# Loads of a fused attention and mixture-of-experts kernel in quarter pieces behind single exponentials, with row stores, list building and one ratio at other units

## The chip, the cores and the metric

One core of one Trainium2 chip. The time is in device microseconds of one execution of the program; lower is better.

## The reference

Attention over 8 batches of 8 heads, 576 positions, 64 dimensions, with rotated q and k; then, with the attention output as 4608 rows of 512, a top-1 mixture of 8 experts. Cut to what matters:

```python
q_rot, k_rot = rotate(q), rotate(k)
scores = scale * q_rot @ k_rot.T
attn = exp(scores - max(scores)); attn /= attn.sum(-1) + 1e-09
x = (attn @ v).transpose(0, 2, 1, 3).reshape(B * S, H * D)
e_idx = argmax(x @ w_gate)                    # one expert for each row
probs = softmax(x @ w_gate); eom = sigmoid(x @ w_output_gate)
out[row] = probs[row, e] * eom[row, e] * (relu(x[row] @ w1[e]) @ w2[e])   # e = e_idx[row]
```

## The kernel before, in words

All inputs are float32. The attention runs over 32 pairs of heads, four for each batch, numbered 0 to 31. A pair has nine units: eight of 128 query rows by one head and one that holds the last 64 rows of both heads. The order of the work is written out by hand as a table of numbers: entry `(name, o, k)` of pair n runs at unit 9n + o, after that unit's exponentials, in place k among those of its unit. No scheduler reorders anything; each engine takes its instructions in the order in which the code issues them.

For a unit, PE makes the scores (tile `sc`, L521), DVE finds the row peak (`peak`, L530, tile `pm`), ACT takes the exponential (`exp`, L537), and DVE transposes (L543, L545, tile `pt`). PE multiplies with the values (`values`, L567, tile `acc`, 144 products for a pair, run one pair later), ACT copies the sums out of PSUM (L574 to L576), PE turns them back (`back`, L582), and DVE divides (`divide`, L594, tile `xb`), which ends the pair's part of one batch's rows. There is one `acc` tile of four PSUM banks.

A pair's inputs come by DMA over SP's queue: `load(1)` and `load(0)` bring the k and the q side of q, k and their half-swapped copies (tile `raw`, 576 KB each, two tiles in turn), `loadv(0)` and `loadv(1)` the values of each head (tile `v`, 576 KB each, two in turn). SP issues a DMA as soon as its tile is free, so the place in the table only sets the order. POOL rotates: two multiplications (`mult`, L472), an addition (`add`, L476), and, after ACT's rounded copy (`high`, L482), the rest (`low`, L485), which completes tile `kq` for the scores two pairs after the loads were due.

After a batch's last pair, `place` routes its rows: POOL sums the gate logits, ACT takes an exponential `eg` (L679) for the ratio by which a row is weighted (s10, s11, s12, s13), PE counts rows in front of each row (s14, L715, in bank 3 of a later pair's `acc`, the "guest" sums), ACT copies the counts out (`rc`, L720), and POOL works out list row and place of each token (s14b to s17: `pr`, `po`, `hr`, `lo`). From these ACT makes row and place matrices (`ones`, tile `ro`, L761 and L762; `places`, tile `pl`, L772 and L773) at the units of `ROWS` and `PLACES`, and PE multiplies them into lists (s20, also in bank 3, columns from 128 on), which ACT copies out (`lc`, L720). Batches 0 to 3 are of kind "free", 4 "late", 5 (the last but two) "early", 6 "ahead"; batch 7 is done in the expert phase. The finished rows go to DRAM (`store`, tile `xd`) over SP's queue, from where the expert phase gathers them.

The expert phase starts near 472 us. Its weights (tile `wr`, 512 KB each, L1098) come over the same SP queue behind the last `loadv`.

The lines of the tables that the change edits:

```python
PREPARED = [("load1", -18, 1), ("load0", -15, 1), ("mult1", -14, 1), ("mult0", -11, 1), ...]
ROWS = {"early": (26, 29, 31, 35, 40), "late": (28, 33, 38, 42, 49), "free": (29, 38, 47, 51, 56), ...}
PLACE = 20   # an entry (o, k) of place runs at unit 9 * (last pair of the batch) + PLACE + o
```

Of the kernel before, what the change touches and what calls it, by code (L numbers as in the profile page):

```python
# [64 lines left out]
ROWS = {"ahead": (26, 29, 29, 31, 31), "early": (26, 29, 31, 35, 40), "late": (28, 33, 38, 42, 49), "free": (29, 38, 47, 51, 56)}  # L65
PLACES = {"ahead": (26, 27, 28, 29, 30), "early": (25, 29, 31, 34, 38), "late": (29, 31, 40, 47, 51), "free": (33, 40, 42, 49, 58)}
# [209 lines left out]
class Attention:  # L276


    def __init__(self, tc, nb, pools, cc, ident, ii, first, trib, oneb, cnt, zero, qk, v, xd, row, lists):
# [33 lines left out]
        for i, pr in enumerate(self.pairs):  # L313
            g, b = 9 * i, i // NP
            fs = {"lasts": pr.lasts, "den0": pr.den0, "den1": pr.den1, "den2": pr.den2, "evict": pr.evict, "back": pr.back,
                  "newxb": lambda pr=pr, b=b: newxb(b) if pr.hp == 0 else None}
            fs["divide"] = lambda pr=pr, b=b: pr.divide(xbs[b])
            for t, n in ((slice(0, 1), "0"), (slice(1, 2), "1"), (slice(0, 2), "")):
                fs[f"mult{n}"] = lambda pr=pr, t=t: pr.mult("P", t)
                fs[f"add{n}"] = lambda pr=pr, t=t: pr.add("P", t)  # L320
                fs[f"hi{n}"] = lambda pr=pr, t=t: pr.high(t)
                fs[f"lo{n}"] = lambda pr=pr, t=t: pr.low("P", t)
            for t in range(2):
                fs[f"load{t}"] = lambda pr=pr, t=t: pr.load(t)
                fs[f"loadv{t}"] = lambda pr=pr, t=t: pr.loadv(t)
# [76 lines left out]
class Pair:  # L402
# [49 lines left out]
    def load(self, t):  # L452

        if t:
            self.raw = self.pp2.tile([P, 4, S], F32, tag="raw", name=f"raw{self.nm}")
        self.nc.sync.dma_start(out=self.raw[:, 2 * t:2 * t + 2, :], in_=self.qkd[:, 2 * t:2 * t + 2, :])

    def loadv(self, t):
# [3 lines left out]
        self.nc.sync.dma_start(out=self.v[:, t, :, :], in_=self.vd[:, t, :, :])  # L462
# [31 lines left out]
    def begin(self):  # L494
        self.pc, self.ps, self.m = {}, {}, {}
# [36 lines left out]
    def exp(self, i):  # L532
# [4 lines left out]
        self.nc.scalar.activation(self.pc[i], self.pc[i], AF.Exp, bias=self.m[i], scale=-1.0, accum_out=self.z[:, zi:zi + 1])  # L537
# [51 lines left out]
    def divide(self, xb):  # L589
# [4 lines left out]
        self.divided = self.nc.vector.tensor_tensor(out=heads(xb[:, :, x0:x0 + BW]), in0=heads(acc), in1=rz.broadcast_to((P, NCH, HW, 2)),  # L594
                                                    op=ALU.mult)
        for m in self.guests:
            self.apart(self.divided, m)

    def apart(self, a, b):

        self.tc.declare_no_dep(a.ins, b.ins, reason="the products stand in banks 0 and 1, the guests' sums in bank 3")

    def guest(self, m):
        self.guests.append(m)


def place(tc, pools, pairs, b, NT, cc, trib, oneb, cnt, xbs, xd, row, lists, tops, later):
# [100 lines left out]
    def psum(k, at, n):  # L708
# [3 lines left out]
        return host.acc[:, 3, at:at + n]  # L712

    def summed(*a, **k):
        m = nc.tensor.matmul(*a, skip_group_check=True, **k)  # L715
        if not last:
            T["host"].guest(m)

    def taken(out, a):
        T["host"].guest(nc.scalar.copy(out, a))  # L720

    def s14():

        rk = T["rk"] = psum(2, 0, (NCH + 1) * E).rearrange("p (a b) -> p a b", b=E)
# [71 lines left out]
    if last:  # L796
# [543 lines left out]
```

## Time and profile before

| | us |
|---|---|
| median of 3 runs | 965.22 |
| the runs | 961.87, 965.65, 965.22 |
| the profiled execution | 961.01 |
| its span | 959.2 |
| PE busy in the span | 911.8 |
| DVE, ACT, POOL busy | 753.4, 658.7, 528.9 |

The span is what the profile's engines cover; the execution's own time is 1.8 us longer. Busy times are sums over instructions; PE's ends are modelled. The profiled execution lies 4.2 us under the median.

### The profile page before, as it was taken

The numbers are of one execution on the slowest core, as the hardware profiler recorded it, in microseconds if no ns is written. First come the engines' busy times: TensorE is split into PE (matmuls) and PEld (weight loads), VectorE is DVE, ScalarE is ACT, GpSimd is POOL, SyncE is SP. The second block draws the span as 40 slices with busy tenths as digits, with TensorE's granted clock in tenths as the row PEclk, the third lists the DMA queues.
The fourth block names the chain that finished last, engine by engine and source line by source line (L and its number), as shares of the span: only waits on it lengthen the run. The fifth ranks groups of instructions, "written<-read, shape, count | busy, mean of one in ns | idle before, by whom it ended". The sixth has DMA issues, their size and how long they took to land.

```text
span 959.2 us, 34178 instructions
## 1 busy us (share of the span) xinstructions
PE 911.8 (95%) x14445; PEld 789.2 (82%) x14445; DVE 753.4 (79%) x1354; ACT 658.7 (69%) x1373; POOL 528.9 (55%) x483
## 2 busy tenths in 40 slices
PE   4999999999999989989899999999999999999997
PEld 3777777878878777777788998999899998999986
DVE  6899999999999989989588776657765757668562
ACT  4777789899998988797764544457645656556562
POOL 5898898898989898797222222142514315042140
PEclk9999999999999999999999999999999999999999
DMA  6554466365636555554299867667876868768560
GB/s 239 199 180 147 178 227 231 142 227 200 245 135 243 203 182 182 177 186 173 97 359 313 304 205 239 219 217 270 290 269 226 292 199 303 255 225 289 198 203 25
DMA packets 57821, 208.42 MB, mean 217 GB/s; under 512 B 7818, under 2 KB 8252, under 8 KB 57664
## 3 DMA queue, kind: packets, MB, share of 16 engines
q1 hardware_dynamic: 49920, 183.78, 54.8%
q0 software_dynamic: 6464, 21.26, 5.9%
q8 instruction: 115, 1.88, 0.8%
q10 hardware_dynamic: 1280, 1.15, 0.4%
q14 instruction: 42, 0.34, 0.1%
HBM read 186.09 MB, written 22.43 MB: 217 GB/s over the span
## 4 chain that ended last, share of the span: by engine, by line
PE 69%; DVE 13%; issue 6%; POOL 5%; ACT 5%; DMA 2%; POOLq 0%; DVEq 0%; SPq 0%; ACTq 0%
PE py L1192 20%; PE ph L1150 19%; PE acc L567 12%; PE sc L521 10%; DVE pm L530 6%; PE ph L1142 3%; DVE pt L545 2%; ACT pm L537 2%; PE acc L582 2%; POOL raw L472 2%; DVE pt L543 2%; PE mtp L1115 2%; POOL kq L485 1%; DVE xb L594 1%; DMA out<-y,2idx 1%
## 5 line engine op out<-in xcount | busy, mean ns | idle before, releaser
L537 ACT ACTIVATE pm<-pm,m 128x576 f32<-128x576 f32 x288 | 221.7, 770 | 55.9 <-DVE pm L530 52.6
L1109 DVE TENSOR_TENSOR wl<-wr,wh 128x1024 fp32r<-128x1024 f32 x172 | 216.2, 1271 | 37.2 <-ACT wh L1107 34.2
L530 DVE TENSOR_SCALAR_CACHE_REDUCE pm<-sc 128x576 f32<-128x576 f32 x288 | 205.1, 744 | 24.4 <-PE sc L521 19.4
L567 PE MATMUL acc<-pt,v 32*64 32x128 f32 (+1 forms) x9216 | 198.5, 295 | 21.2 <-issue 9.2
L1192 PE MATMUL py<-wh,ht 128*128 128x512 f32 x640 | 214.0, 400 | 0.0
L1150 PE MATMUL ph<-xt,wh 128*128 128x256 f32 x1088 | 198.3, 284 | 0.0
L567 PEld LDWEIGHTS acc<-pt,v 32*64 32x64 f32 x9216 | 157.5, 131 | 47.6 <-issue 29.7
L1107 ACT CAST wh<-wr 128x1024 fp32r<-128x1024 f32 x184 | 187.8, 1049 | 0.0
L521 PE MATMUL sc<-kq 64*128 64x288 f32 x1536 | 159.8, 320 | 15.4 <-ACT kq L482 9.6
L1150 PEld LDWEIGHTS ph<-xt,wh 128*128 128x128 f32 x1088 | 169.8, 190 | 2.6 <-DVE xt L1131 1.2
L472 POOL TENSOR_TENSOR raw<-raw,rt 128x1152 f32<-128x1152 f32 x62 | 164.8, 2658 | 0.0
L521 PEld LDWEIGHTS sc<-kq 64*128 64x128 f32 x1536 | 121.5, 190 | 48.7 <-issue 20.8
L1150 PE MATMUL ph<-xt,wl 128*128 128x256 f32 x544 | 154.0, 283 | 0.0
L1192 PEld LDWEIGHTS py<-wh,ht 128*128 128x128 f32 x640 | 120.3, 188 | 25.2
L1192 PE MATMUL py<-wl,ht 128*128 128x512 f32 x320 | 125.8, 393 | 0.0
L543 DVE STREAM_TRANSPOSE pt<-pm 128x576 f32<-128x576 f32 x160 | 116.7, 759 | 2.1 <-ACT pm L537 2.1
L1166 ACT ACTIVATE ht<-ph 128x512 fp32r<-128x512 f32 x68 | 40.7, 598 | 112.9 <-PE ph L1150 103.3
L1197 POOL DMA_INDIRECT out<-y,2idx x24 | 26.0, 1083 | 166.1 <-ACT y L1206 104.7
L1167 DVE SCALAR_TENSOR_TENSOR ht<-ph,ht 128x512 fp32r<-128x512 f32 x68 | 47.0, 691 | 73.7 <-ACT ht L1166 70.3
L1150 PEld LDWEIGHTS ph<-xt,wl 128*128 128x128 f32 x544 | 103.0, 189 | 0.2 <-DVE wl L1109 0.2
L545 DVE STREAM_TRANSPOSE pt<-pm 128x1152 f32<-128x1152 f32 x64 | 87.9, 1373 | 0.7 <-ACT pm L537 0.7
L485 POOL TENSOR_TENSOR kq<-raw,kq 128x1152 fp32r<-128x1152 f32 (+1 forms) x33 | 82.8, 2509 | 8.7 <-ACT kq L482 8.5
(243 smaller groups left out, 1105.0 us busy)
## 6 DMA issues: line engine op xcount, KB each, us to landing
wr<-in_w SPq DMA_DIRECT2D x184, 512.0 KB, 4.4
raw<-in_qk SPq DMA_DIRECT2D x64, 576.0 KB, 5.2
v<-in_v SPq DMA_DIRECT2D x64, 576.0 KB, 6.1
xd<-xb SPq DMA_DIRECT2D x16, 640.0 KB
xd<-xb SPq DMA_DIRECT2D x8, 160.0 KB, 5.1
rt<-in_rope ACTq DMA_DIRECT2D x1, 576.0 KB
xg<-xd,2idx POOLq DMA_INDIRECT x24, 6.7
out<-y,2idx POOLq DMA_INDIRECT x24, 3.4
```

Source lines behind the costliest of these rows:

```text
L472: self.eng(eng).tensor_tensor(out=rv, in0=rv, in1=rt, op=ALU.mult)
L485: self.eng(eng).tensor_tensor(out=self.sides(self.kq, t, 0, x), in0=self.sides(self.raw, t, 0, x), in1=self.sides(self.kq.bitcast(F32), t, ...
L521: self.nc.tensor.matmul(self.ps[i][:, a, :HS], st, self.kq[r, mov, x], start=(n == 0), stop=(n == 2))
L530: self.nc.vector.tensor_scalar(self.halves(i), self.ps[i][:, :, :HS], 1.0, FAR, op0=ALU.mult, op1=ALU.min, accum_out=self.m[i])
L537: self.nc.scalar.activation(self.pc[i], self.pc[i], AF.Exp, bias=self.m[i], scale=-1.0, accum_out=self.z[:, zi:zi + 1])
L543: self.nc.vector.transpose(out=self.pt[:, c + 5 * h, :], in_=self.pc[units[0]])
L545: self.nc.vector.transpose(out=self.pt[:, c:c + 6:5, :], in_=self.pc[units])
L567: nc.tensor.matmul(self.acc[h * D:h * D + D, a, o:o + 32 * n], self.v[r, h, j, :], self.pt[r, u:u + n, 32 * j:32 * j + 32], start=(j == 0) ...
L1107: self.nc.scalar.copy(wh, r)
L1109: eng.tensor_tensor(out=wl, in0=r, in1=wh.bitcast(F32), op=ALU.subtract)
L1150: nc.tensor.matmul(ph[:, f, :], st[:, dc, fs], mv[:, dc, :], start=(n == 0), stop=(n == 11))
L1192: self.nc.tensor.matmul(py[h], st[:, f, hs], mv, start=(f == 0 and n == 0), stop=(f == 7 and n == 2))
```

## The change

Loads: `raw` and `v` now come in four pieces of 288 KB each in place of two of 576 KB. Piece t of pair n's `raw` waits for the exponential of unit t of pair n - 2 (k side first), piece t of its `v` for the exponential of unit t + 4 of pair n itself. The three row stores of a batch stand together at PLACE + 33, between a pair's last `v` piece and the next `raw` pieces, and the ratio is written into the rows (s13) at PLACE + 24 in one instruction in place of two. One `ro` chunk of the "free" batches moves from 51 to 31, `pl` chunks of "late" from 47 and 51 to 45 and 47, those of "early" to other units. The lists' sums stand in PSUM bank 2, the counts in bank 3, and the two are declared independent. For batch 5 POOL works out `pr`, `po`, `hr` and `lo` directly after the counts and the ratio behind them.

```diff
+LOADED = [(f"load{t}", t - 18, 2) for t in range(4)]
+PREPARED = [*LOADED, ("mult1", -14, 1), ("mult0", -11, 1), ("add", -9, 1), ("hi", -6, 1), ("lo", -5, 2)]
 EVENTS = [
-    ("lasts", 1, 2), ("loadv0", 5, 2), ("loadv1", 7, 2),
+    ("lasts", 1, 2), *[(f"loadv{t}", t + 4, 2) for t in range(4)],
...
-ROWS = {"ahead": (26, 29, 29, 31, 31), "early": (26, 29, 31, 35, 40), "late": (28, 33, 38, 42, 49), "free": (29, 38, 47, 51, 56)}
-PLACES = {"ahead": (26, 27, 28, 29, 30), "early": (25, 29, 31, 34, 38), "late": (29, 31, 40, 47, 51), "free": (33, 40, 42, 49, 58)}
+ROWS = {"ahead": (26, 29, 29, 31, 31), "early": (22, 24, 29, 33, 38), "late": (28, 33, 38, 42, 49), "free": (29, 31, 38, 47, 56)}
+PLACES = {"ahead": (26, 27, 28, 29, 30), "early": (22, 27, 31, 35, 40), "late": (29, 31, 40, 45, 47), "free": (33, 40, 42, 49, 58)}
...
+                fs[f"load{t}"] = lambda i=i, pr=pr, t=t: pr.load(t, self.pairs[i - 2].ex[t])
+                fs[f"loadv{t}"] = lambda pr=pr, t=t: pr.loadv(t, pr.ex[t + 4])
...
+    def behind(self, dma, ex):
+        if ex is not None:
+            info = mybir.DependencyInfo(mybir.DependencyClass.Sync, mybir.DependencyReason.DATA)
+            self.tc.add_manual_dep(dma.ins, ex.ins.name, info, reason="transfers evenly in time")
+    def load(self, t, ex=None):
+        if t == 0:
             self.raw = self.pp2.tile([P, 4, S], F32, tag="raw", name=f"raw{self.nm}")
-        self.nc.sync.dma_start(out=self.raw[:, 2 * t:2 * t + 2, :], in_=self.qkd[:, 2 * t:2 * t + 2, :])
+        t ^= 2
+        self.behind(self.nc.sync.dma_start(out=self.raw[:, t, :], in_=self.qkd[:, t, :]), ex)
...
-    def guest(self, m):
-        self.guests.append(m)
+    def guest(self, m, bank):
+        for o, k in self.guests:
+            if k != bank and o.ins.engine != m.ins.engine:
+                self.apart(m, o)
+        self.guests.append((m, bank))
...
-        rk = T["rk"] = psum(2, 0, (NCH + 1) * E).rearrange("p (a b) -> p a b", b=E)
+        rk = T["rk"] = psum(2, 3, (NCH + 1) * E).rearrange("p (a b) -> p a b", b=E)
...
-        T["ls"] = psum((listed + PLACE) // 9 - 2, 128, lists.shape[1])
+        T["ls"] = psum((listed + PLACE) // 9 - 2, 2, lists.shape[1])
...
+    ratio = lambda: (s10(), s11())
+    if early:
+        fs += [(18, 2, s14b), (18, 2, s15), (19, 2, s16), (19, 2, s17), (20, 2, ratio), (22, 2, s12)]
+    else:
+        fs += [(19, 2, ratio), (19, 2, s14b), (20, 2, s15), (21, 2, s12), (22, 2, s16), (23, 2, s17)]
...
-        fs += [(29, 2, lambda: gated(0, 2)), (33, 2, lambda: store(0)), (38, 2, lambda: gated(2, NCH)),
-               (42, 2, lambda: store(1)), (42, 2, lambda: store(2))]
+        fs += [(24, 2, s13), (33, 2, lambda: store(0)), (33, 2, lambda: store(1)), (33, 2, lambda: store(2))]
```

SP's queue around the row stores of batch 0. Before, a transfer waits only for its tile (`Pool`: POOL has finished with the `raw` tile, `PE`: the values before are used) and for the semaphore of an earlier transfer (`DMAHW`); a tile's number is the program's own:

```order
L462 DMA v_2469<-in_v 128x1152 [waits DMAHW3_49,DMAHW2_49,PE_49]
L462 DMA v_2469<-in_v 128x1152
L700 DMA xd<-xb_584 128x2x640 [waits DMAHW4_49,Pool_49]
L456 DMA raw_2575<-in_qk 128x1152 [waits DMAHW5_49,Pool_49]
L456 DMA raw_2575<-in_qk 128x1152 [waits DMAHW6_49]
L462 DMA v_2760<-in_v 128x1152 [waits DMAHW7_49,PE_49]
L462 DMA v_2760<-in_v 128x1152 [waits DMAHW0_49]
L700 DMA xd<-xb_584 128x2x640 [waits DMAHW1_49,Pool_49]
```

and after, where `Activation` is the exponential:

```order
L472 DMA v_2437<-in_v 128x576 [waits DMAHW0_49,Activation_49]
L472 DMA v_2437<-in_v 128x576 [waits DMAHW1_49,Activation_49]
L713 DMA xd<-xb_594 128x2x640 [waits DMAHW2_49,Pool_49]
L713 DMA xd<-xb_594 128x2x640 [waits DMAHW3_49]
L715 DMA xd<-xb_594 64x640 [waits DMAHW4_49]
L465 DMA raw_2619<-in_qk 128x576 [waits DMAHW5_49,Activation_49,Pool_49]
L465 DMA raw_2619<-in_qk 128x576 [waits DMAHW6_49,Activation_49]
L465 DMA raw_2619<-in_qk 128x576 [waits DMAHW7_49,Activation_49]
```

What ran ahead on free tiles now waits for ACT piece by piece, and the three stores stand in one row.

PE at the unit where batch 4's lists (`ro`, `pl`) and batch 5's counts (`hot`) are summed. Before:

```order
L715 MATMUL acc_7682<-ro_7139,pl_7174 128x288 x4
L715 MATMUL acc_7682<-ro_7139,pl_7174 128x288 [waits Activation_49]
L715 LDWEIGHTS trib
L715 MATMUL acc_7682<-hot,trib 128x48 [waits Activation_49]
L715 LDWEIGHTS oneb
L715 MATMUL acc_7682<-hot,oneb 128x40
```

and after:

```order
L729 MATMUL acc_7787<-ro_7236,pl_7272 128x288 x5
L729 LDWEIGHTS trib
L729 MATMUL acc_7787<-hot,trib 128x48
L729 LDWEIGHTS oneb
L729 MATMUL acc_7787<-hot,oneb 128x40
```

The order is the same; the counts' wait for ACT (the copy `lc`) is gone, and so is that of the last list product for its `pl`.

POOL after batch 5's counts, the copy `rc`. Before:

```order
L737 TENSOR_TENSOR pr_8036<-rc_7962,base_7645 128x40
L738 TENSOR_TENSOR cnt<-rc_7962,cnt 128x8
L682 TENSOR_SCALAR eg_7990<-eg_7990 128x5
L685 TENSOR_TENSOR eg_7990<-eg_7990,so_7913 128x5
L792 TENSOR_TENSOR lists<-lists,lc_7954 128x288
L472 TENSOR_TENSOR raw_7940<-raw_7940,rt 128x1152
L741 TENSOR_TENSOR pr_8036<-pr_8036,hot 128x40
L485 TENSOR_TENSOR kq_8033<-raw_7641,kq_8033 128x2x576
```

and after:

```order
L755 TENSOR_TENSOR pr_8098<-pr_8098,hot 128x40
L643 TENSOR_TENSOR po_8146<-pr_8098 128x20
L643 TENSOR_TENSOR po_8148<-po_8146 128x10
L643 TENSOR_TENSOR po_8150<-po_8148 128x5
L763 TENSOR_SCALAR hr_8152<-po_8150 128x5
L764 TENSOR_SCALAR hr_8152<-hr_8152 128x5
L765 TENSOR_SCALAR hr_8152<-hr_8152 128x5
L766 TENSOR_SCALAR lo_8153<-hr_8152 128x5
L767 TENSOR_TENSOR lo_8153<-lo_8153,po_8150 128x5
L806 TENSOR_TENSOR lists<-lists,lc_8059 128x288
L482 TENSOR_TENSOR raw_8047<-raw_8047,rt 128x1152
L695 TENSOR_SCALAR eg_8096<-eg_8096 128x5
```

`lo` stood behind three large POOL instructions and the wait for ACT's `eg`; it now stands ahead of both.

## Rows read from the trace of the kernel before

**Rows 1.** windows between divides; PE, PEld, DVE, ACT, POOL busy, clock, DMA.

```profile
234.69:289.22 54.53, 52.33 (x1422) 43.46 (x1421) 52.95 (x112) 49.58 (x129) 49.96 (x46) 1.00 0.57 205
344.32:376.07 31.75, 27.52 (x714) 22.25 (x715) 26.83 (x57) 25.41 (x66) 28.29 (x23) 1.00 0.67 230
376.07:421.94 45.87, 40.50 (x1073) 33.12 (x1071) 40.11 (x85) 39.33 (x103) 37.84 (x43) 1.00 0.48 172
480.00:504.00 24.00, 24.00 (x161) 21.55 (x160) 19.75 (x36) 14.64 (x21) 4.96 (x4) 1.00 0.95 358
```

**Rows 2.** chain of work, two divides; start us, us, engine, tile, line.

```profile
71.51 0.89 DVE xb L594
...
84.89 0.89 DVE xb L594
```

**Rows 3.** waits of PE, 60 to 340 us; total us, times, longest.

```profile
PE acc L567 <- ACT rc L720: 3.5, 5, 0.8
...
PE acc L567 <- issue: 0.3, 1, 0.3
```

**Rows 4.** waits of PE from 340 to 425 us.

```profile
PE acc L567 <- issue: 6.1, 5, 1.5
...
PE acc L715 <- ACT lc L720: 1.2, 1, 1.2
```

**Rows 5.** page, part 3, instruction queue; packets, MB, share.

```profile
q8 instruction: 115, 1.88, 0.8%
```

**Rows 6.** DMA queues, 344 to 349 us.

```profile
q1 hardware_dynamic: 375, 1.54, 83.8%
```

**Rows 7.** DMA queues, 349 to 351 us.

```profile
q1 hardware_dynamic: 38, 0.14, 17.9%
q8 instruction: 1, 0.02, 3.0%
```

**Rows 8.** chain of work, 350 to 358 us.

```profile
350.95 0.85 issue
```

**Rows 9.** timelines of DVE, ACT; start us, us, instruction [idle <- who].

```profile
279.49 0.76 DVE L530 TENSOR_SCALAR_CACHE_REDUCE pm<-sc 128x576 f32<-128x576 f32 x1 [0.56 <-PE sc L521]
...
392.37 0.76 DVE L530 TENSOR_SCALAR_CACHE_REDUCE pm<-sc 128x576 f32<-128x576 f32 x1 [1.96 <-PE sc L521]
...
406.57 0.40 ACT L772 ACTIVATE pl<-row,lo 128x128 fp32r<-128x128 bf16 x1 [1.19 <-POOL lo L753]
```

**Rows 10.** waits of POOL from 24 to 336 us.

```profile
POOL eg L682 <- ACT eg L679: 10.0, 5, 2.3
...
POOL pr L737 <- ACT rc L720: 4.7, 5, 1.4
```

**Rows 11.** timelines, ACT (second exponential, pair 18), POOL (first multiplication, pair 20).

```profile
262.06 0.76 ACT L537 ACTIVATE pm<-pm,m 128x576 f32<-128x576 f32 x1
...
263.04 2.65 POOL L472 TENSOR_TENSOR raw<-raw,rt 128x1152 f32<-128x1152 f32 x1
```

**Rows 12.** page, part 6 (us to landing); one store, its window.

```profile
raw<-in_qk SPq DMA_DIRECT2D x64, 576.0 KB, 5.2
...
351.27 0.38 SPq L700 DMA_DIRECT2D xd<-xb  x1
...
352.00:354.20 2.20, 2.20 (x76) 1.81 (x73) 1.49 (x4) 1.98 (x7) 2.20 (x2) 1.00 0.79 297
```

**Rows 13.** end of the attention: timelines of SP and ACT, then the chain.

```profile
447.99 34.17 SPq L1098 DMA_DIRECT2D wr<-in_w  x10
...
459.34 0.78 ACT L537 ACTIVATE pm<-pm,m 128x576 f32<-128x576 f32 x1 [0.49 <-DVE pm L530]
...
468.33 2.95 ACT L1107 CAST wh<-wr 128x1024 fp32r<-128x1024 f32 x3
...
466.94 0.85 issue
...
470.21 1.87 issue
```

More of the change, by code (lines that the diff above doesn't have):

```diff
@@ L43 @@
 NB, TAIL, PE_ = S // 32, 160, 192
-PREPARED = [("load1", -18, 1), ("load0", -15, 1), ("mult1", -14, 1), ("mult0", -11, 1), ("add", -9, 1), ("hi", -6, 1), ("lo", -5, 2)]
+LOADED = [(f"load{t}", t - 18, 2) for t in range(4)]
+PREPARED = [*LOADED, ("mult1", -14, 1), ("mult0", -11, 1), ("add", -9, 1), ("hi", -6, 1), ("lo", -5, 2)]
 EVENTS = [
-    ("lasts", 1, 2), ("loadv0", 5, 2), ("loadv1", 7, 2),
+    ("lasts", 1, 2), *[(f"loadv{t}", t + 4, 2) for t in range(4)],
     ("av0", 12, 1), ("av1", 13, 0), ("av2", 14, 0), ("av3", 16, 0),
@@ L56 @@
     1: (("mult1", -9, 1), ("add1", -9, 1), ("mult0", -8, 1), ("add0", -7, 1), ("hi1", -5, 1), ("lo1", -4, 1), ("hi0", -3, 1), ("lo0", -2, 1)),
[1 row of a table removed]
+    2: (*LOADED, ("mult1", -11, 1), ("add1", -10, 1), ("mult0", -9, 1), ("add0", -7, 1), ("hi1", -6, 1),
         ("lo1", -5, 1), ("hi0", -4, 1), ("lo0", -3, 1)),
[1 row of a table removed]
+    3: (*LOADED, ("mult1", -11, 1), ("mult0", -9, 1), ("add", -7, 1), ("hi", -4, 1), ("lo", -4, 2)),
 }
@@ L322, in __init__ @@
                 fs[f"lo{n}"] = lambda pr=pr, t=t: pr.low("P", t)
-            for t in range(2):
-                fs[f"load{t}"] = lambda pr=pr, t=t: pr.load(t)
-                fs[f"loadv{t}"] = lambda pr=pr, t=t: pr.loadv(t)
+            for t in range(4):
+                fs[f"load{t}"] = lambda i=i, pr=pr, t=t: pr.load(t, self.pairs[i - 2].ex[t])
+                fs[f"loadv{t}"] = lambda pr=pr, t=t: pr.loadv(t, pr.ex[t + 4])
             for k, (b0, b1) in enumerate(PIECES):
@@ L357, in start @@
             f()
-        self.pairs[1].load(1)
-        self.pairs[1].load(0)
+        for t in range(4):
+            self.pairs[1].load(t)
         self.pairs[0].start()
@@ L450, in eng, with loadv @@
         return self.nc.gpsimd if eng == "P" else self.nc.vector
-    def load(self, t):
-        if t:
+    def behind(self, dma, ex):
[4 more added lines that the diff above has]
+        if t == 0:
             self.raw = self.pp2.tile([P, 4, S], F32, tag="raw", name=f"raw{self.nm}")
-        self.nc.sync.dma_start(out=self.raw[:, 2 * t:2 * t + 2, :], in_=self.qkd[:, 2 * t:2 * t + 2, :])
-    def loadv(self, t):
+        t ^= 2
+        self.behind(self.nc.sync.dma_start(out=self.raw[:, t, :], in_=self.qkd[:, t, :]), ex)
+    def loadv(self, t, ex):
         if t == 0:
             self.v = self.pa.tile([P, 2, NB, D], F32, tag="v", name=f"v{self.nm}")
-        self.nc.sync.dma_start(out=self.v[:, t, :, :], in_=self.vd[:, t, :, :])
+        h, j = t // 2, slice(t % 2 * 9, t % 2 * 9 + 9)
+        self.behind(self.nc.sync.dma_start(out=self.v[:, h, j, :], in_=self.vd[:, h, j, :]), ex)
     def sides(self, a, t, s, x):
@@ L494, in begin @@
     def begin(self):
-        self.pc, self.ps, self.m = {}, {}, {}
+        self.pc, self.ps, self.m, self.ex = {}, {}, {}, {}
         self.pt = self.pa.tile([P, 9, S], F32, tag="pt", name=f"pt{self.nm}")
@@ L536, in exp @@
             zi = 2 * c + h
-        self.nc.scalar.activation(self.pc[i], self.pc[i], AF.Exp, bias=self.m[i], scale=-1.0, accum_out=self.z[:, zi:zi + 1])
+        self.ex[i] = self.nc.scalar.activation(self.pc[i], self.pc[i], AF.Exp, bias=self.m[i], scale=-1.0, accum_out=self.z[:, zi:zi + 1])
     def turn(self, units):
@@ L593, in divide @@
         heads = lambda a: a.rearrange("p c (x h) -> p c x h", h=2)
[L594 to L597, printed above, removed]
+        divided = self.nc.vector.tensor_tensor(out=heads(xb[:, :, x0:x0 + BW]), in0=heads(acc), in1=rz.broadcast_to((P, NCH, HW, 2)),
+                                               op=ALU.mult)
+        for m, _ in self.guests:
+            self.apart(divided, m)
     def apart(self, a, b):
-        self.tc.declare_no_dep(a.ins, b.ins, reason="the products stand in banks 0 and 1, the guests' sums in bank 3")
-    def guest(self, m):
-        self.guests.append(m)
+        self.tc.declare_no_dep(a.ins, b.ins, reason="the products stand in banks 0 and 1, lists' sums in bank 2, counts in bank 3")
+    def guest(self, m, bank):
[3 more added lines that the diff above has]
+        self.guests.append((m, bank))
 def place(tc, pools, pairs, b, NT, cc, trib, oneb, cnt, xbs, xd, row, lists, tops, later):
@@ L705, in base, with psum @@
         tt(out=new("base", [P, E]), in0=cnt, in1=cc(C_EB), op=ALU.add)
-    def psum(k, at, n):
+    def psum(k, bank, n):
         if last:
@@ L711, in psum @@
         host = T["host"] = pairs[NP * b + NP - 1 + k]
-        return host.acc[:, 3, at:at + n]
+        T["bank"] = bank
+        return host.acc[:, bank, 0:n]
     def summed(*a, **k):
@@ L716, in summed @@
         if not last:
-            T["host"].guest(m)
+            T["host"].guest(m, T["bank"])
     def taken(out, a):
-        T["host"].guest(nc.scalar.copy(out, a))
+        T["host"].guest(nc.scalar.copy(out, a), T["bank"])
     def s14():
-        rk = T["rk"] = psum(2, 0, (NCH + 1) * E).rearrange("p (a b) -> p a b", b=E)
+        rk = T["rk"] = psum(2, 3, (NCH + 1) * E).rearrange("p (a b) -> p a b", b=E)
         mm = lambda out, st, mv, start, stop: summed(out, st, mv, start=start, stop=stop)
@@ L802, in place @@
     fs = [(0, 2, s0), (2, 2, s1), (2, 3, s2), (7, 2, base), (8, 2, s3), (10, 2, s4), (11, 2, s5), (12, 2, s7), (15, 2, s8), (17, 2, s14),
-          (17, 2, s14c), (19, 2, s14b), (18, 2, s9), (19, 2, lambda: (s10(), s11())), (20, 2, s15), (21, 2, s12), (22, 2, s16), (23, 2, s17)]
+          (17, 2, s14c), (18, 2, s9)]
+    ratio = lambda: (s10(), s11())
[3 more added lines that the diff above has]
+        fs += [(19, 2, ratio), (19, 2, s14b), (20, 2, s15), (21, 2, s12), (22, 2, s16), (23, 2, s17)]
     fs += [(listed, 2, s20), (listed, 2, s21), (listed + 1, 2, s22) if early else (listed + 2, 3, s22)]
```

2 rows, old and new, of the table PREP are left out of this document.

## The prediction

> **What bounds the kernel now.** I read the stretches first, then PE's waits, then the queues at each wait. Both phases run at the full clock [rows 1]: TensorE's granted clock is 1.00 of 2.4 GHz, so nothing here is a matter of the clock. From 480 to 504 us PE is busy in 24.00 of 24.00 us: the expert phase is bound by PE's own work, and the change adds nothing to that work and takes nothing from it. A gain or a loss must come from the attention, or from the change-over near 470 us.
>
> In the attention a pair takes 84.89 - 71.51 = 13.38 us where nothing is lost [rows 2]. An ordinary batch of four pairs takes 54.53 us, 13.63 a pair, with PE busy 52.33 and DVE 52.95 us: these two are nearly full. The five pairs from 344.32 to 421.94 take 31.75 + 45.87 = 77.62 us where five times 13.63 is 68.15 [rows 1]. So 9.5 us are lost in this stretch; PE is busy 27.52 + 40.50 = 68.0 of its 77.6 us. Where they go:
>
> - PE waits 6.1 us, in five waits of up to 1.5, for "issue", that is for nothing that the profile shows; from 60 to 340 us that was 0.3 us in all [rows 3, 4]. I take these for waits on PE's own instructions, which come by a DMA queue too: 115 packets and 1.88 MB in the run, 16 KB each [rows 5]. From 344 to 349 us the data queue alone fills 83.8% of the DMA engines and not one instruction packet moves; from 349 to 351 us, when the data fall to 17.9%, one does [rows 6, 7]; PE stops at 350.95 for 0.85 us, just as it has come in [rows 8].
> - PE waits 1.2 us to count rows into `acc`, for ACT's copy `lc` out of the same bank [rows 4]; DVE, which waits for the scores queued behind, is idle 1.96 us at 392.37 [rows 9].
> - ACT waits 1.19 us at 406.57 with a `pl` for POOL's `lo` [rows 9].
>
> 6.1 + 1.96 + 1.19 = 9.25, about the 9.5.
>
> **The change part by part.** The sum goes from the profiled execution, 961.0 us, and is moved to the median afterwards.
>
> Loads. The bytes stay. What changes is when they move: eight pieces of 288 KB behind one exponential each, in place of four transfers of 576 KB that start together as tiles come free. A 640 KB store issued by itself at 351.27 moves at 297 GB/s in the 2.20 us to 354.20 [rows 12], so a piece, by size, is 1.0 us of transfer. An instruction packet then stands behind one or two pieces, not behind 6 us. **+6.1 us** if every such wait goes, nothing if the fetch was not the cause; and **-2.0 us**, an estimate, for short waits that remain or appear at other places (bounds 0 and 4, a piece's time four times). The four loads more for a pair cost SP some 0.38 us of issue each [rows 12], and SP has only issues to do: nothing, as long as it does not stand in a wait while a tile further down is needed.
>
> What the loads lose is their lead. POOL's first multiplication of pair 20 begins at 263.04, and the exponential that the last k-side piece will wait for (unit 1 of pair 18) ends at 262.06 + 0.76 = 262.82 [rows 11], 0.2 us earlier. POOL now waits for that piece there. The landing time L, from the exponential's end, lies between 1.7 us (the store's 2.93 from its issue to the end of its data, less 352 KB at its own rate) and 5.2 us, the median for `raw` on the page, where transfers stand in line [rows 12]. I take 2.7, nearer the store, since pieces seldom stand in line. So POOL starts 2.5 us later once in four pairs. In each batch it now waits 10.0 / 5 + 4.7 / 5 = 2.9 us for ACT's `eg` and `rc` [rows 10], in work that is queued behind this multiplication, so lateness up to about 3 us goes into waits that are there anyway. Taken: **-1.0 us** for six batches together; bounds nothing and 6 x (5.2 - 0.2 - 3.0) = 12.
>
> The bank. With counts in bank 3 and lists in bank 2, PE no longer waits for `lc`: **+1.9 us** by what DVE was idle (bounds 1.2, PE's wait, and 1.96).
>
> Batch 5's order. `lo` comes ahead of two large POOL instructions, so `pl` finds it ready: **+1.0 us** (bounds 0 and 1.19). What moves behind it, the ratio, is needed only when the rows are written.
>
> The other units. One `ro` of each of batches 0 to 3 leaves the unit in which ACT makes the copy `rc`. PE waits 3.5 us in five places for `rc` [rows 3], and at 279.49 this left DVE idle 0.56 us [rows 9]. **+2.0 us**: four batches at 0.5; bounds 0, if the copy is late for other work of ACT's, and 3.5. The ratio in one POOL instruction saves a fixed cost on an engine with slack: nothing. The three stores, 1.44 MB, take 4.8 us at the rate of [rows 12], and the next `raw` pieces stand in line with them; that is a `raw` of a batch's last pair, not of its first, where the multiplication starts closest, so I price it at nothing, and up to the 5.2 us of L without that cover.
>
> The end. The ten weight transfers stand behind the last `v` pieces on SP: today they start at 447.99, after the change not before the last pair's exponentials, of which one starts at 459.34; I put it at 461.5. The first that uses a weight is ACT's cast at 468.33 [rows 13], 6.8 us later, enough for the landing. But PE waits for "issue" at 466.94 and 470.21, 0.85 and 1.87 us [rows 13], and the weights will now move densely just there. **-1.7 us**, one such wait more; bounds none and two, 3.4.
>
> The sum: 6.1 - 2.0 + 1.9 + 1.0 + 2.0 - 1.0 - 1.7 = 6.3, or 954.7 for the profiled execution. That execution is 4.2 us under the median, 965.22; I move half of this, since the runs lie on both sides: **956.8 us**.
>
> **A rule against it.** The row is that not one instruction packet moved while the data queue ran from 344 to 349 us [rows 6]; by it the 6.1 us come back when the data are spread. The Trainium skill, DMA: Bandwidth & Descriptors, section "Queues, rings and completion order", has each DMA engine take turns between queues packet by packet, so a fetch would wait for a packet and not for a burst. Its page Runtime: NRT & Kernel Launch, section "Instruction fetch mechanics", calls the cost of the next block of instructions mostly hidden, since the fetch runs ahead of execution. By these two the issue waits would not be fetches held up by data, and the time would be that of the first rival; the trace speaks against them at the wait that is shown [rows 8].
>
> **The rivals.**
>
> *The issue waits stay.* PE takes its instructions late for another reason (the matmuls' own records, or a fetch that is asked for late), and spreading data does nothing for it. For this: waits of this kind also stand at 466.94 and 470.21, where the data are not those of a pair. Against it: [rows 6 to 8]. The sum loses 6.1 and the 2.0 that went with it: a gain of 2.2, 958.8, or 960.9 on the median's footing. Chance 0.12.
>
> *POOL becomes late, and the kernel slower.* If pieces land L after their exponential, a batch costs L - 0.2 - 3.0, in six batches. For it: the start of the multiplication is 0.2 us behind the exponential [rows 11], and POOL is busy 49.96 of 54.53 us [rows 1], so it does not catch up. Against it: spread transfers seldom queue. Without POOL's term the forecast is 955.8; 965.22 is reached at L = 3.2 + 9.4 / 6 = 4.8 us, and at the page's 5.2 the time is 955.8 + 12 = 967.8. Slower by over 0.5% needs 5.6. Chance 0.14, most of it within 0.5%.
>
> *All of these waits vanish*, and no new one comes: 6.1 + 1.9 + 1.0 + 3.5 = 12.5, so 948.5, or 950.6. Chance 0.08.
>
> **How the numbers follow.** A measurement of this kernel tells about 0.5% from no change, 4.8 us: faster is under 960.4, slower over 970.0. The forecast has 0.66; its own range, from the small bounds of -2.0 and +2.0 to their large ones, is 953 to 960.5, so nearly all of it is faster, 0.64. Of "the issue waits stay" 0.05 is faster and 0.07 the same; of POOL's case 0.10 is the same and 0.04 slower; 0.08 of the last is faster. Together 0.77, 0.19 and 0.04. The range leaves out most of POOL's case above and half of the last below: 950 to 963.
>
> **What would show it.** In the profile after: PE's `acc` waits for "issue" from 340 to 425 us fall from 6.1 to about 2, instruction packets move between pieces, and the five pairs take under 71 us. PE's wait for `lc` and ACT's for `lo` are gone, and those for `rc` from 60 to 340 us are about half. POOL's first multiplication of a batch's first pair waits about 2.5 us for a DMA, and its waits for `eg` and `rc` shrink by as much; if they reach nothing and the pitch of an ordinary batch is over 54.53, the second rival holds. The weights are issued after 461 us and the issue waits near 470 grow by about 1.7. Issue waits as long as before with the loads spread would make the prediction wrong in its main step; a batch pitch that grows would make it wrong on the lead.

## The result: slower by 0.9%

The changed kernel takes 970.85 us (median of 20 runs, 966.41 to 974.85) beside 961.69 of the kernel before in 20 runs: a ratio of 1.0094, interval 1.0078 to 1.0109. The forecast was 956.8 (950 to 963), from a median of 965.22 for before; further runs of before put it lower, at 960 to 962. The profiled execution of the changed kernel spans 972.8 us, 13.6 more than that of before; it lies 3.8 above its median, so the sizes read from the traces are somewhat larger than the 9.2 us between the medians.

The windows of the changed kernel, between the same divides in both (columns as in [rows 1]; the last of them in the expert phase):

```profile
84.67:313.84 229.17, 216.19 (x5677) 178.19 (x5675) 213.09 (x445) 192.01 (x496) 199.25 (x180) 0.99 0.63 189
313.84:429.37 115.53, 107.65 (x2844) 88.25 (x2842) 106.72 (x224) 102.15 (x267) 98.35 (x99) 1.00 0.64 195
...
429.37:492.25 62.88, 54.53 (x1383) 45.80 (x1380) 45.99 (x93) 43.34 (x109) 36.15 (x62) 0.95 0.48 153
...
240.47:299.26 58.79, 54.72 (x1420) 45.44 (x1419) 53.41 (x112) 49.69 (x129) 49.53 (x45) 0.97 0.62 189
...
357.47:386.36 28.89, 27.25 (x714) 22.32 (x715) 26.57 (x56) 26.33 (x68) 24.34 (x17) 1.00 0.69 218
386.36:429.37 43.01, 40.84 (x1071) 33.48 (x1070) 40.12 (x85) 38.41 (x103) 38.11 (x46) 1.00 0.61 184
...
493.00:517.00 24.00, 24.00 (x160) 21.54 (x159) 19.68 (x37) 14.59 (x20) 4.94 (x4) 1.00 0.97 357
```

and three of the kernel before:

```profile
84.81:303.10 218.29, 209.60 (x5677) 173.81 (x5675) 211.85 (x445) 190.82 (x494) 198.18 (x182) 1.00 0.55 197
303.10:421.94 118.84, 107.18 (x2844) 87.86 (x2842) 106.74 (x224) 102.91 (x267) 102.55 (x102) 1.00 0.55 193
421.94:478.80 56.86, 51.87 (x1385) 43.95 (x1382) 45.55 (x92) 43.09 (x110) 32.95 (x62) 0.97 0.39 140
```

Three things are to be seen. Four batches in which before lost little (16 pairs) are 229.17 - 218.29 = 10.9 us longer. The eight pairs behind them are 118.84 - 115.53 = 3.3 us shorter, and the five pairs that had lost 9.5 us take 28.89 + 43.01 = 71.9 us where they took 77.62 [rows 1]. The last four pairs are 6.0 us longer. Together they make up the 13.6 us. The expert phase is bound by PE in both. The batch of 54.53 us in [rows 1] takes 58.79 us, 4.3 more, and its clock is 0.97; it holds the longest of the 16 pairs, so the other three batches lost less.

PE's waits in the changed kernel, from 340 to 425 us (first row, [rows 4]) and from 60 to 340 (the other three, [rows 3]), then POOL's from 24 to 336 ([rows 10]):

```profile
PE acc L577 <- issue: 1.3, 4, 0.4
```

```profile
PE sc L531 <- POOL kq L495: 7.4, 5, 2.9
...
PE acc L577 <- issue: 2.7, 7, 0.7
...
PE acc L577 <- ACT rc L734: 0.5, 1, 0.5
```

```profile
POOL raw L482 <- DMA raw<-in_qk: 27.9, 11, 5.4
...
POOL eg L695 <- ACT eg L692: 4.0, 3, 2.0
```

What the change was meant to do happened: the issue waits of 6.1 us are 1.3, those for `rc` are 0.5 in place of 3.5, and the one for `lc` and ACT's for `lo` are gone. From 60 to 475 us the issue waits at `acc` are 4.7 us in place of 9.2. But POOL waits 27.9 us for `raw`, and PE 7.4 us for `kq`, rows that did not exist.

**Where the time went, in one batch.** SP, POOL, PE and the windows of the changed kernel behind a divide at 254.45, where the row stores of batch 2 go out:

```profile
246.32 5.21 SPq L472 DMA_DIRECT2D v<-in_v  x4
251.62 0.91 SPq L713 DMA_DIRECT2D xd<-xb  x2
252.58 2.64 SPq L715 DMA_DIRECT2D xd<-xb  x1
255.33 2.81 SPq L465 DMA_DIRECT2D raw<-in_qk  x4
```

```profile
q1 hardware_dynamic: 1428, 3.12, 90.0%
q8 instruction: 1, 0.02, 0.9%
...
raw<-in_qk SPq DMA_DIRECT2D x4, 288.0 KB, 6.3
```

```profile
257.04 0.32 POOL L660 TENSOR_TENSOR lgs<-h 128x80 f32<-128x80 f32 x1
262.75 2.64 POOL L482 TENSOR_TENSOR raw<-raw,rt 128x1152 f32<-128x1152 f32 x1 [5.39 <-DMA raw<-in_qk]
265.36 2.61 POOL L495 TENSOR_TENSOR kq<-raw,kq 128x1152 fp32r<-128x1152 f32 x1
```

The same two instructions of POOL in the kernel before, without a wait:

```profile
251.32 2.68 POOL L472 TENSOR_TENSOR raw<-raw,rt 128x1152 f32<-128x1152 f32 x1
...
254.08 2.66 POOL L485 TENSOR_TENSOR kq<-raw,kq 128x1152 fp32r<-128x1152 f32 x1
```

PE in the changed kernel, and windows around its wait:

```profile
264.68 0.40 PE L531 MATMUL sc<-kq 64*128 64x288 f32 x2
268.02 1.57 PE L531 MATMUL sc<-kq 64*128 64x288 f32 x10 [2.94 <-POOL kq L495]
269.51 2.51 PE L592 MATMUL acc<-ii,ac 128*128 128x160 f32 x10
```

```profile
265.00:268.30 3.30, 0.36 (x4) 0.28 (x4) 0.89 (x2) 2.38 (x7) 3.30 (x4) 0.95 0.40 111
268.30:272.06 3.76, 3.76 (x22) 3.31 (x21) 2.13 (x5) 1.64 (x5) 3.68 (x2) 0.59 0.02 4
```

The three stores (L713, L715) stand ahead of the four `raw` pieces of pair 19 in SP's queue. From 253 to 262.7 us the queue moves 3.12 MB almost without a break, 90.0% of the DMA engines: what is left of the `v` pieces, the 1.44 MB of stores, and behind them the `raw` pieces, 6.3 us from issue to landing. POOL's multiplication (L482) waits 5.39 us for them. Behind it on POOL stands L495, the `low` of pair 18, whose inputs are long there and whose scores are due: PE waits 2.94 us for it. Then the clock falls: the window behind the wait has 0.59, and ten turning products take 2.51 us where they take 1.63 at the full clock. The pair takes 17.61 us, from 254.45 to 272.06; in the kernel before it took 13.38. This is the worst of the places: the pairs in which the stores of batches 0, 1, 3 and 4 go out are longer by 1.0, 2.9, 2.4 and 0.1 us. The multiplications behind the other batches' stores wait 3.9 to 4.9 us; these five waits are 22.5 of the 34.9 us that POOL waits for `raw` up to 475 us.

**The end**, in PE's timeline of the changed kernel (what follows the two `issue` waits), then of the kernel before (the turning products at the full clock, then what follows the first `issue`):

```profile
479.59 4.05 PE L577 MATMUL acc<-pt,v 32*64 32x128 f32 x128 [1.88 <-issue]
485.52 0.77 PE L577 MATMUL acc<-pt,v 32*64 32x128 f32 x24 [1.88 <-issue]
```

```profile
461.10 1.63 PE L582 MATMUL acc<-ii,ac 128*128 128x160 f32 x10 [1.04 <-ACT ac L576]
...
467.79 2.43 PE L567 MATMUL acc<-pt,v 32*64 32x128 f32 x128 [0.85 <-issue]
```

The weights go out at 472.41 us. The two fetch waits are 1.88 and 1.88 us where they were 0.85 and 1.87 [rows 13], and 128 products behind the first take 4.05 us and not 2.43, at the lower clock: 1.03 + 1.62 = 2.65 us, which is the difference of the last pair (18.70 us from divide to divide and 16.04). The other 3.4 us of the last four pairs' 6.0 lie in the three pairs ahead of it, mostly in two of 14.79 and 15.56 us that were 13.38 and 13.82; what delays these is not taken apart.

### The profile page after: what moved, and what is told of

The parts are those of the page before. It is cut to its first block, busy times and chain, and to the rows that moved or that the text cites. A ratio compares the mean times of both kernels' runs of the same rounds, so it can differ in the third digit from the quotient of the medians.

```text
span 972.8 us, 34538 instructions
## 1 busy us (share of the span) xinstructions
PE 921.6 (95%) x14445; PEld 795.7 (82%) x14445; DVE 755.1 (78%) x1354; ACT 659.4 (68%) x1373; POOL 524.9 (54%) x477
## 3 DMA queue, kind: packets, MB, share of 16 engines
q8 instruction: 115, 1.88, 0.8%
## 4 chain that ended last, share of the span: by engine, by line
PE 45%; issue 4%; DVE 1%; DMA 1%; POOL 1%; ACT 1%; POOLq 0%; ACTq 0%; DVEq 0%
PE py L1210 20%; PE ph L1168 19%; PE ph L1160 3%; PE mtp L1133 2%; PE acc L577 1%; DMA out<-y,2idx 1%; PE acc L592 0%; PE htp L1195 0%; DVE wl L1127 0%; ACT wh L1125 0%; PE sc L531 0%; DVE pm L540 0%; POOL kq L495 0%; POOL wl L1127 0%; POOLq L1289 0%
## 5 line engine op out<-in xcount | busy, mean ns | idle before, releaser
L1127 DVE TENSOR_TENSOR wl<-wr,wh 128x1024 fp32r<-128x1024 f32 x172 | 216.3, 1271 | 37.6 <-ACT wh L1125 34.9
L577 PE MATMUL acc<-pt,v 32*64 32x128 f32 (+1 forms) x9216 | 201.2, 297 | 16.8 <-issue 8.5
L531 PE MATMUL sc<-kq 64*128 64x288 f32 x1536 | 165.8, 323 | 25.8 <-POOL kq L495 10.0
L482 POOL TENSOR_TENSOR raw<-raw,rt 128x1152 f32<-128x1152 f32 x62 | 164.6, 2655 | 36.4 <-DMA raw<-in_qk 34.9
L531 PEld LDWEIGHTS sc<-kq 64*128 64x128 f32 x1536 | 124.2, 192 | 62.4 <-issue 19.9
L495 POOL TENSOR_TENSOR kq<-raw,kq 128x1152 fp32r<-128x1152 f32 (+1 forms) x33 | 82.4, 2500 | 5.7 <-ACT kq L492 5.7
```

The costliest lines, as they stand in the source:

```text
L482: self.eng(eng).tensor_tensor(out=rv, in0=rv, in1=rt, op=ALU.mult)
L495: self.eng(eng).tensor_tensor(out=self.sides(self.kq, t, 0, x), in0=self.sides(self.raw, t, 0, x), in1=self.sides(self.kq.bitcast(F32), t, ...
L531: self.nc.tensor.matmul(self.ps[i][:, a, :HS], st, self.kq[r, mov, x], start=(n == 0), stop=(n == 2))
L577: nc.tensor.matmul(self.acc[h * D:h * D + D, a, o:o + 32 * n], self.v[r, h, j, :], self.pt[r, u:u + n, 32 * j:32 * j + 32], start=(j == 0) ...
L1127: eng.tensor_tensor(out=wl, in0=r, in1=wh.bitcast(F32), op=ALU.subtract)
```

## The experiments

Each ratio is to the kernel before on the same chip, with its interval behind it. It is not the quotient of the two medians; the two differ by up to 0.14%. Kernels that ran on different chips are compared by their ratios.

**1. Stores at other places in SP's queue.** Two kernels move the stores and nothing else, and two take one part of the change alone. The entries of the table, with the code around the stores left out:

```diff
 changed            (24, 2, s13), (33, 2, store(0)), (33, 2, store(1)), (33, 2, store(2))
-stores apart       (24, 2, s13), (33, 2, store(0)), (42, 2, store(1)), (42, 2, store(2))
+stores after raw   (24, 2, s13), (37, 2, store(0)), (37, 2, store(1)), (37, 2, store(2))
```

Stores at the units of before:

> The changed kernel with its three row stores at the units of before (one at PLACE + 33, two at PLACE + 42). Theory A (the raw pieces behind three stores in one row come late, POOL waits 3.9 to 5.4 us for them five times, and the low part that stands behind on POOL makes the scores late): the DMA waits at those multiplications fall below 2.5 us, the stretch of the five batches gets some 5 us shorter, about 966 us. Theory B (the lead given up by waiting for an exponential costs the time wherever the stores stand): within 2 us of the changed kernel, 969 to 972.

Measured: 978.52 us, ratio 1.0185 (1.0126 to 1.0244). Worse, which neither theory expected. DVE's waits and, from SP's timelines, the second and third store of batch 2, in this kernel and in before:

```profile
DVE xb L604 <- DMA xd<-xb: 16.2, 6, 4.0
```

```profile
259.58 5.19 SPq L472 DMA_DIRECT2D v<-in_v  x4
264.83 0.42 SPq L713 DMA_DIRECT2D xd<-xb  x1
```

```profile
254.16 0.38 SPq L700 DMA_DIRECT2D xd<-xb  x1
```

DVE's divide waits 16.2 us, six times, for a store to leave the `xb` tile that the next batch needs. A place in the table is only an order: in before SP ran ahead to it on free tiles, at 254.16, 5.75 us behind the divide of pair 15; behind gated pieces the same place is reached at 264.83, 10.72 us behind that divide. So the gates delay every transfer that stands behind them in the queue.

Stores behind the raw pieces:

> The changed kernel with the three row stores together at PLACE + 37, behind the four raw pieces of the next pair and ahead of its v pieces, in place of PLACE + 33, ahead of the raw pieces. The transfers and their waits are the same, only the row in the queue changes. Theory A: POOL's waits of 3.9 to 5.4 us for raw go, the losses of the batches with stores (9.9 us in the four batches 98 to 299 us, by the pitch) go with them, about 961 us. Theory B: 969 to 972.

Measured: 964.1 us, ratio 1.0036 (1.0012 to 1.0061). Theory A holds for the larger part, 0.58% of the 0.94; POOL's longest wait for `raw` is 2.1 us in place of 5.4, and PE's waits for `kq` from 60 to 475 us are 1.0 us in place of 9.5.

Loads alone, on the kernel before:

> The kernel before with the loads in pieces behind exponentials and nothing else; its stores stay apart (PLACE + 33 and + 42). Theory A: issue waits from 340 to 425 us fall to 1 to 2 us, POOL waits little for raw, and the time is 956 to 961. Theory B: POOL waits for raw in every batch and the time is 966 or more.

Measured: 989.95 us, ratio 1.0293 (1.0239 to 1.0347), missed by far: with the stores at their old units the divide waits for `xb` here too, 16.8 us in six places. That is not all of the 28.8 us lost; the rest is not taken apart. With the stores left where they were, the spread loads lose far more than the changed kernel does.

The rest alone, without loads and stores:

> The kernel before with the bank, the units of ROWS and PLACES and batch 5's order changed, the loads and the stores left as before. By the prediction's terms 1.9 + 1.0 + 2.0 = 4.9 us faster than before, 956.8 beside 961.7; the issue waits of 340 to 425 us stay near 6 us. If those waits follow the data bursts only loosely, they move to other places. The rival, that these terms are off the path, has it within 1.5 us of before.

Measured: 958.66 us beside 961.2, ratio 0.9986 (0.996 to 1.0012): not the 4.9 us. Its PE waits, 340 to 425 us and then 60 to 475:

```profile
PE acc L569 <- issue: 4.0, 4, 1.1
```

```profile
PE acc L569 <- issue: 10.6, 14, 2.1
...
PE acc L569 <- ACT rc L726: 0.3, 1, 0.3
```

The waits for `rc` and `lc` went as forecast, but PE's issue waits fell at the five places only from 6.1 to 4.0 and came up elsewhere, 10.6 us in all.

**2. Gates, and what they are for.**

Coarse loads with the stores together:

> The changed kernel with the loads as before (two transfers of 576 KB per tile, waiting only for the tile), the three stores together at PLACE + 33 and all other edits kept. Theory A in its narrow form (three stores in a row hurt only because the raw pieces behind them are gated, so that they have no lead to lose): POOL hardly waits for raw, within 2 us of the same kernel with stores apart, 957 to 961. If three stores in a row hurt by themselves: 965 or more with POOL waiting for raw in five places.

Measured: 962.41 us, ratio 1.0023 (1.0002 to 1.0044): POOL has no wait for `raw` in its list, so three stores in a row hurt POOL only when the loads behind them are gated. The time is 1.4 us above the range given, and the ratio 0.37% above that of the kernel with these loads and the stores apart (0.9986), with intervals that overlap: whether the three stores cost something by another way is open.

Pieces, but no gate (`behind` does nothing):

> The changed kernel with its pieces of 288 KB and its three stores together, but no piece waits for an exponential. Theory F (the fetch waits come from data in one burst, and the gates, not the smaller size, cure them): in 340 to 425 us the issue waits are back to 4 us or more, from 1.3; POOL hardly waits for raw, and the time is near that of the coarse loads with stores together, 962.4: 960 to 964. If the size of the pieces is what counts, the issue waits stay near 1.3 and the time is 956 to 959.

Measured: 968.58 us, ratio 1.0074 (1.005 to 1.0099), more than either theory gave. The waits come out as theory F says; PE's waits from 340 to 425 us, one of them, and windows behind it:

```profile
PE acc L577 <- issue: 4.3, 2, 2.6
```

```profile
358.34 1.32 PE L577 MATMUL acc<-pt,v 32*64 32x128 f32 x56 [1.70 <-issue]
```

```profile
360.00:361.00 1.00, 1.00 (x12) 1.00 (x10) 0.00 (x0) 0.19 (x1) 1.00 (x1) 0.50 0.33 69
361.00:362.00 1.00, 1.00 (x28) 0.72 (x34) 0.58 (x1) 0.00 (x0) 1.00 (x1) 0.50 0.79 226
```

Halving the transfers alone does nothing for the issue waits (from 60 to 475 us 12.9 us at `acc` here, 14.2 with the coarse loads and the stores together, 4.7 in the changed kernel); making the pieces wait does. The wait shown also costs the clock: 1.70 us of standing, and 0.50 from 360 us on. The mean clock from 60 to 475 us is 0.98 here and 1.00 with the coarse loads, which is part of the 6 us between the two; the rest is not taken apart.

**3. The lead, and the end.** On the kernel with the stores behind the raw pieces: the last pair's `v` pieces free, raw pieces two units earlier, both, and both with four units.

```diff
-                fs[f"loadv{t}"] = lambda pr=pr, t=t: pr.loadv(t, pr.ex[t + 4])
+                fs[f"loadv{t}"] = lambda i=i, pr=pr, t=t: pr.loadv(t, pr.ex[t + 4] if i < 31 else None)
...
+SOONER = [(f"load{t}", t - 18 - 2, 2) for t in range(4)]
...
+                fs[f"load{t}"] = lambda i=i, pr=pr, t=t: pr.load(t, self.passed(9 * (i - 2) + t - (2 if i > 2 else 0)))
```

> The kernel with the stores behind the raw pieces (964.1 us), and the last pair's four v pieces wait for no exponential, so that the weights behind them on SP are issued near 447 us as before and not at 460. Theory C (the weights' burst then falls on the last two instruction fetches: waits of 2.6 and 1.8 us in place of 0.9 and 1.9, and after the first PE runs 128 products in 4.10 us in place of 2.43): the last pair takes 16 us in place of 19.4, 960.7 us. The rival, that the late weights cost nothing and something else made the last pair long: 964.

Measured: 960.54 us, ratio 1.0012 (0.9993 to 1.0031), from 1.0036; the last pair takes 15.75 us. As theory C has it by the time and by the pair (19.43 us before), though the intervals of the two ratios overlap.

> The kernel with the stores behind the raw pieces (964.1 us), each raw piece waiting for the exponential two units earlier and the stores one unit earlier, still behind the last raw piece. Theory D (what remains against the coarse loads is lead: POOL waits 23.0 us in 16 places for raw, and its additions end just when the cast wants them): those waits fall under 5 us, 960 to 962. Rival E (no lead is wanted, POOL's waits are covered by its slack): 963 to 965.

Measured: 960.78 us, ratio 0.9992 (0.9969 to 1.0015). The time is theory D's; its sign is not, for 15.5 us of DMA waits are left on POOL in 8 places, where under 5 were foretold.

> Both edits, the last pair's v pieces free and the raw pieces two units earlier: if theories C and D both hold, 957 to 959, which is faster than before (961.2) by 0.3 to 0.5% and level with the kernel of coarse loads and the other edits (958.7). If only C holds, 960 to 961.

Measured: 958.5 us, ratio 0.9995 (0.9971 to 1.0019): in the range of both theories by the time, but not below the kernel with one edit by the ratio. The two don't add up to anything that shows.

> The kernel with both edits (last pair's v pieces free, raw pieces earlier), with the raw pieces four units earlier in place of two and the stores still behind the last of them (PLACE + 34). Theory D: POOL's waits for raw, 13.2 us in 8 places with two units, fall under 5, and the time is 956 to 958. If instead the fetch waits set what is left, POOL's waits go and the time does not: 958 to 960.

Measured: 961.87 us, ratio 1.0015 (0.9992 to 1.0038). POOL's waits for `raw` are 4.1 us and the time doesn't fall; it lies above both ranges. More lead is worth nothing beyond two units, and whether it was lead that the two units gave is not shown. PE's issue waits from 43 to 484 us are 9.0 us here, 7.7 with two units.

**4. POOL's queue.** One number: the first multiplication of a pair behind the `low` of the pair before, not ahead of it.

```diff
-PREPARED = [*LOADED, ("mult1", -14, 1), ("mult0", -11, 1), ("add", -9, 1), ("hi", -6, 1), ("lo", -5, 2)]
+PREPARED = [*LOADED, ("mult1", -14, 3), ("mult0", -11, 1), ("add", -9, 1), ("hi", -6, 1), ("lo", -5, 2)]
```

> The changed kernel with one number changed: a pair's first multiplication stands behind the low part of the pair before on POOL's queue, not ahead of it. Loads, gates and stores are as in the changed kernel. Theory G (the late raw pieces cost time because the low part, whose scores are due, stands behind the multiplication that waits for them): PE's 9.5 us of waits for kq from 60 to 475 us fall under 3, the losses of the batches 98 to 299 us go, and the time is 962 to 965. Rival H (the late pieces make their own pair's rotation late, wherever the low part stands): 969 to 971.

Measured: 960.07 us, ratio 1.0004 (0.9986 to 1.0022), from 1.0094: more than theory G asked for. POOL's largest wait from 20 to 475 us, and PE's, 60 to 475:

```profile
POOL kq L495 <- ACT kq L492: 23.3, 22, 4.0
```

```profile
PE acc L577 <- issue: 9.6, 13, 2.2
PE acc L577 <- DVE xb L604: 6.9, 16, 0.5
```

No wait for `raw` and none of PE for `kq` is left in these lists. The stores, the gates and the late pieces are those of the changed kernel; rival H falls. How much of the gain theory G may claim, the next kernel shows.

> The kernel before with the one exchange on POOL (a pair's first multiplication behind the low part of the pair before). Theory G: in this kernel the multiplication never waits for its raw tile, so the exchange frees nothing; within 2 us of before, 959 to 963. Rival K (the exchange is a gain by itself, and the changed kernel's loss was not about the late pieces): 955 or less.

Measured: 957.22 us beside 961.48, ratio 0.9952 (0.9931 to 0.9973). Neither theory: the exchange is a gain by itself, 0.48%, about half of the 0.90% that it brought in the changed kernel. If the changed kernel's gain contains the same part, 0.42%, some 4 us, is left for the wait behind the late pieces. With the exchange in both, the changed kernel is still 0.52% behind (1.0004 and 0.9952). Where the kernel before gains, PE's waits from 340 to 425 us show:

```profile
PE acc L567 <- issue: 0.2, 1, 0.2
```

They are 0.2 us, with no load spread, where before had 6.1 [rows 4]. `low` is the last that reads a `raw` tile; when it runs sooner, the tile is free and its load issued at another time. That this is what moves the fetches out of the bursts' way is argued, not shown.

> The changed kernel with the exchange on POOL (960.1 us) and the last pair's v pieces waiting for no exponential, so that the weights are issued some 12 us earlier. Theory C: the last pair takes 15 to 16 us in place of 17.4, 957 to 959. If the long last pairs have another cause, 960 to 961.

Measured: 957.82 us, ratio 0.9966 (0.9945 to 0.9987); the last pair takes 14.1 us, even less than the 15 to 16 foretold. Theory C holds, and the kernel is 0.14% behind the one above (0.9952) on the same chip, inside the intervals: what the exchange leaves of the changed kernel's loss goes for the most part with the late weights.

> The kernel with both edits (958.5 us: stores behind the raw pieces, raw pieces two units earlier, last pair's v pieces free) and the same exchange on POOL. Theory G: the DMA waits of POOL that remain, 13.2 us in 8 places, lose what cost they have left, 956 to 958. If POOL's order no longer matters once the pieces are early, 958 to 959; if the low part now waits for its cast ahead of work that was ready, 960 or more.

Measured: 962.29 us, ratio 1.0013 (0.999 to 1.0036): no better than without the exchange, and in the range of the last case. POOL's `low` waits 23.1 us for its cast, but it waits 23.3 us in the changed kernel with the exchange, which gained; so why nothing is gained here stays open.

> The kernel before with the exchange on POOL (957.2 us beside 961.5) and the bank, the units of ROWS and PLACES and batch 5's order as in the changed kernel; loads and stores as before. If those edits' waits (4.0 us for rc, 1.2 for lc, 1.2 for lo) lie on the path, 953 to 955. If they are hidden or fetch waits come in their place, 956 to 958.

Measured: 955.82 us beside 961.82, ratio 0.9937 (0.9909 to 0.9964), the best version: loads and stores of before, POOL's exchange, and the changed bank, units and order. The time lies between the two ranges, and the gain over the exchange alone, 0.15%, is inside the intervals.

## Why the prediction was wrong

The step that failed is the sentence on the stores: "the next `raw` pieces stand in line with them; that is a `raw` of a batch's last pair, not of its first, where the multiplication starts closest, so I price it at nothing". The sentence goes on to name up to 5.2 us, but neither the sum nor the range took them in. The line and the pair are as they were foretold: pair 19 is a batch's last. The price was looked for at the wrong instruction. I asked when the pieces' own pair needs them, and not what stands behind the multiplication on POOL: the `low` of the pair before, due in 2 us (in the kernel before it ended at 256.74, and PE began the scores that need it at 258.62). The prediction's own method, to name what is queued behind a waiting instruction, was used on the first pair of a batch alone. The stores cost 0.58% by their place in SP's queue (experiment 1), about 5.6 us, and the exchange of POOL's two rows gained 0.42%, some 4 us, more in the changed kernel than in the kernel before (experiment 4): the two agree on the size.

This step alone does not make the miss. The sum was a gain of 6.3 us, the medians show a loss of 9.2, 15.5 us apart. Beside the 5.6 of the stores, the three small terms fell short by some 3.6 us, and the late weights cost 2.3 to 3.7 us in place of 1.7 (the points below). The 4 to 6 us left, an estimate, are about the gain that was expected of the issue waits; no run gives that part by itself.

Point by point:

- **Issue waits, +6.1 and -2.0.** Right in the stretch from 340 to 425 us: 1.3 us were left, and the ungated pieces brought 4.3 back, so the rival that they stay is not borne out. The eight pairs from 313.84 gained 3.3 us in all. As a gain of the whole it is not shown: from 60 to 475 us the waits fell from 9.2 us to 4.7 at `acc`, but the kernel with POOL's exchange has 4.5 without a spread load. Two readings were too strong. From 60 to 340 us PE also waited 1.0 us for "issue" with `sc`, so it was 1.3 us in all and not 0.3. And from 344 to 349 us the answer behind [rows 6] also has `q14 instruction: 1, 0.01, 0.9%`: a packet of another instruction queue did move, and only q8 had none. The Trainium skill's rule of DMA engines that take turns between queues packet by packet (DMA: Bandwidth & Descriptors, "Queues, rings and completion order") is not refuted by these runs. The waits came back with the ungated pieces, but the packet of q8 in the window from 253 to 262.7 us shown above moved while the data filled 90.0% of the engines, which agrees with it. When PE asks for a packet the traces don't show.
- **The lead, -1.0.** The mechanism was right and the place wrong. Where no stores stand in line, pieces landed about 3.2 us behind their exponential (2.7 was taken, and up to 3.2 was free), and from 146 us on the first pairs' multiplications waited 0.2 to 0.9 us. Three others with no stores ahead of them, at 75.28, 103.95 and 421.04, waited 3.0, 4.3 and 2.9. The 3.9 to 5.4 us stood at the last pairs. The rival "POOL becomes late" came true by the stores, and its 2.0 us a batch at L = 5.2 were 4.3 in the batch shown.
- **Bank, order, units: 1.9 + 1.0 + 2.0 = 4.9.** The waits went; the kernel with these three alone gained 0.14% (-0.12 to 0.40), about 1.3 us. Issue waits came up at other places (10.6 us from 60 to 475, where before had 9.2); that these took the rest back is argued, not shown.
- **The end, -1.7.** Right in kind: the two waits grew by 1.03 us. The clock behind them, another 1.62, had no term. Weights issued earlier gave 0.24% back on the kernel with the stores behind the raw pieces and 0.38% on the one with the exchange, with intervals that overlap in the first and just touch in the second: 2.3 to 3.7 us where 1.7 was priced.
- **The clock.** "Nothing here is a matter of the clock" was right of the windows of [rows 1] and not of the change-over: before has 0.97 from 421.94 to 478.80 us, and 0.60 from 472.10 to 476.00, right behind its fetch wait of 1.87 us. In the changed kernel the wait of 2.94 us shown is followed by 0.59.

## What to carry to other kernels

When a transfer is made to wait, look down two queues: what stands behind it among the transfers, and what stands behind its reader on the reader's engine. A step whose inputs are ready and whose result is due goes ahead of the step that waits for a transfer. And a place in a queue that an engine reaches early, because it runs ahead, is no longer early when the entries ahead of it get waits: what relied on that, like the stores here, must move too.

## What the runs showed of the hardware

- Long waits of PE for its instructions can stand behind a full data queue. In the kernel with ungated pieces there are seven such waits of 0.7 to 2.6 us from 60 to 475 us, and each ends 1.2 to 1.5 us after a packet of the instruction queue q8 has come in. In the 2 us ahead of these packets the DMA engines are busy by a share of 0.96 and more for six of them and 0.71 for one, where the mean from 60 to 475 us is 0.57. The packet itself moves in 0.9 to 1.0 us, so it is late and not slow; whether it is held up or asked for late the traces don't show. In the kernel before, the same share for the five waits from 340 to 425 us is 0.62, 0.77, 0.95, 0.22 and 0.65, with a mean of 0.54: there the link is loose.
- A short stop of PE can cost as much again through the clock: 1.70 us of standing in the kernel with ungated pieces, then a granted clock of 0.50 (1.2 GHz, the lower level) in the windows shown from 360 to 362 us. But in the kernel with POOL's exchange 128 products behind a fetch wait of 2.21 us took 2.43 us, as without a wait, and in the changed kernel 4.05 behind 1.88; what decides between the two these runs don't show.
